# Top-32 attention with a PReLU MLP on one core: when pairs are prepared, how the MLP is paced, and two transposes moved from DMA to TensorE

## The chip, the core and the metric

The kernel runs on one core of a Trainium2 chip. A core has five engines with a queue each, which run in order and wait for each other through semaphores: TensorE (PE, matmul; its weight loads are listed as PEld), VectorE (DVE), ScalarE (ACT), GpSimd (POOL) and SyncE (SP, which here only issues DMAs). SBUF is the working memory, PSUM the small memory into which PE writes. The metric is the device time of one execution in microseconds (us); lower is better.

## What is computed

The reference is sparse attention followed by a two-layer MLP, all with random inputs:

```python
# q, k, v: (8 batches, 8 heads, 576 rows, 64)
scores = q @ k.T / sqrt(64)
kth = 32nd largest score of the row
scores = where(scores >= kth, scores, -1e9)
x = softmax(scores) @ v                      # -> (4608 tokens, 512)
h = x @ w_in                                 # (512, 2048)
g = maximum(h, 0) + alpha * minimum(h, 0)
out = g @ w_out                              # (2048, 512)
```

## The kernel before

**Pairs, row blocks, ticks.** Two heads of a batch form a pair; there are 32 pairs (four to a batch). A pair has nine row blocks of 128 score rows: four times 128 rows of each head and one block that holds the last 64 rows of both. That makes 288 row blocks. The program is one long list written out by hand (`manual_schedule`): a loop over ticks `n`, one row block to a tick, and each tick appends instructions to the five queues in a fixed order. Functions put into a calendar with `put(tick, engine, f)` are appended when the loop gets there (`run`). In the last four pairs (from tick 252) the row blocks are interleaved over the pairs, so that a chunk of 128 rows is complete for all heads of the batch early.

**A row block's way.** PE multiplies q and k (`ps`, L314), one unit of two row blocks at a time and a tick ahead. ACT copies the scores with a bias (`b`, L323), counts signs (`h`, L329) and takes the exponential (`e`, L334). POOL makes a sign word (`SG`, L339), DVE a keyed copy (`y`, L345) whose largest eight of each of six segments it finds (`C`, L355) and merges (`L`, L370 and L372). Seven ticks after its scores DVE compares the row with its limit (`mk`, L419), POOL multiplies mask and exponential (`w`, L429), and SP issues a transpose by DMA (`wT<-w`, L442). The last six row blocks use one fused DVE instruction instead (L426). PE multiplies `wT` with v (`pu`, L488), DVE takes the reciprocal of the row sums (`rz`, L505, or L534 in the last batch), and ACT, or DVE in the last batch, scales the result into `xb`. A DMA transpose (`x_turn`, L551) makes `xT`, the MLP's input.

**Preparation.** Before a pair's first row block its q, k and v are loaded (`load`, `load_v`, on SP's queue) and `prep_plan` spreads 17 steps over about 16 ticks ahead of `BASE[p]`: PE transposes q and k (`pq`, `pk`, `pt`), forms k's products (`pg`) and a statistic (`pr`, `st`), with ACT copies between them (`qkT`, `GK`) and DVE steps behind them (`P`, L226, and `sq`, L251 on). `BASE[p]` is 9p for the first 28 pairs, and 247, 250, 254 and 258 for the last four.

**MLP.** PReLU is split into a Relu part and a linear part, so that the second layer is `relu(h) @ (w_out * (1 - alpha)) + x @ (w_in @ (w_out * alpha))`. The matrix in the second term (`w_id_b`) is made once, by four bursts of 16 matmuls (`pl`, L596) and four ACT copies (L600). Tokens are taken in blocks of 512 or 128. A block is a list of steps in the deque `back`: `ph` steps (four matmuls of 512 columns each, or 16 of 128, L635) with an ACT Relu (L641), and `pz` steps, three to 128 tokens (20 matmuls in all, L649 and L653) with an ACT copy (L658) and a DMA out. A step's PE part goes into one tick and its ACT part to the head of the next. Up to tick 251 every tick takes one step; from tick 252 on a credit of 1.9 a tick (2.4 from tick 288) is spent at 0.9 for a `ph` and 1.5 for a `pz` step. `feed` appends a batch's blocks eight ticks after its last weights.

**The end.** After the last row block the remaining chunks of the last batch pass through `av_last`, `rz_last`, `out_last` and `x_turn`, and their MLP steps are appended to `back` two ticks after that.

Of the kernel before, what the change touches and what calls it, by code (L numbers as in the profile page):

```python
# [9 lines left out]
FP32 = mybir.dt.float32  # L10
BF16 = mybir.dt.bfloat16
# [5 lines left out]
S = 576  # L17
# [13 lines left out]
def kernel(  # L31
# [10 lines left out]
    nc = tc.nc  # L42
    B, H, S_, D = q.shape
# [5 lines left out]
    NPAIR = (B * H) // 2  # L49
# [15 lines left out]
    nc.gpsimd.memset(warm, 0.0)  # L65
    nc.scalar.activation(warm, warm, AF.Exp, scale=1.0)
    make_identity(nc, ident_f)
    ones_f = const.tile([128, 1], FP32, name="ones_f")
    nc.gpsimd.memset(ones_f, 1.0)
    bones = const.tile([128, 2], BF16, name="bones")  # L70
# [86 lines left out]
    while n < NT:  # L157
# [2 lines left out]
            unit_of[n + i] = (n, m, i)  # L160
        units.append((n, m))
        n += m
    BASE = {p: TPP * p for p in range(P0)}
    BASE.update({P0: N0 - 5, P0 + 1: N0 - 2, P0 + 2: N0 + 2, P0 + 3: N0 + 6})

    def prep_plan(p):
        d = pairs[p]
# [253 lines left out]
    def weights(n, fused):  # L421
        p, j = ORDER[n]
        d, t = pairs[p], tiles.pop(n)
        dst = w_dst(n)
        if fused:
            nc.vector.scalar_tensor_tensor(out=dst, in0=t["b"], scalar=row_limit(n),  # L426
                                           in1=t["e"], op0=ALU.is_ge, op1=ALU.mult)
        else:
            nc.gpsimd.tensor_tensor(dst, t["mk"], t["e"], ALU.mult)  # L429
        if j == 8:  # L430
            d["wTm"] = prep.tile([128, 9, 128], BF16, name="wT", bufs=6)
            if fused:
                nc.vector.tensor_copy(d["wm"][:, S:640], d["wm"][:, 0:64])
            else:
                nc.gpsimd.tensor_tensor(d["wm"][:, S:640], t["mk"][:, 0:64], t["e"][:, 0:64],
                                        ALU.mult)
            nc.sync.dma_start_transpose(d["wTm"][:, 0:5, :], d["wm"])
            nc.sync.dma_start_transpose(d["wTm"][:, 5:9, :], d["wm"][:, 64:S])
        elif j % 2 == 1:
            wT = prep.tile([128, 9, 128], BF16, name="wT", bufs=6)  # L440
            d["wT", j // 2] = wT
            nc.sync.dma_start_transpose(wT, d["w2"])  # L442

    DDs, xb, xm = {}, {}, {}

# [91 lines left out]
    def out_last(i, g):  # L537
# [4 lines left out]
            dst[:, 256 * g:256 * g + 256].rearrange("p (s d) -> p s d", s=4), pu[0:m, :, 0:D],  # L542
            rz[0:m, 0:4].unsqueeze(2).to_broadcast([m, 4, D]), ALU.mult)

    def x_turn(b, chunks):
        for i in chunks:
            c0 = (b * S + 128 * i) % NX
            if b == B - 1:
                c0 = b * S % NX + (64 + 128 * i if i < 4 else 0)
            if i < 4:  # L550
                nc.sync.dma_start_transpose(xT[:, :, c0:c0 + 128], xb[b][:, i, :])  # L551
            else:
                nc.sync.dma_start_transpose(xT[:, :, c0:c0 + 64], xm[b])

    def weight_steps():
        hold = {}

        def alpha():
            a16 = mlp.tile([NFT, 128], FP32, name="a16", bufs=1)
            nc.sync.dma_start(a16, moe_alpha.rearrange("(t p) -> t p", p=128))  # L560
            hold["a16"] = a16

        def alpha1():
            aps = ps_m.tile([128, NFT], FP32, name="aps", tag="misc")
            nc.tensor.transpose(aps, hold["a16"], ident_f[0:NFT, 0:NFT])
            hold["aps"] = aps
            hold["inT"] = mlp.tile([128, NKT, NFT, 128], BF16, name="w_inT", tag="gT", bufs=1)

        def alpha2():
            nc.scalar.copy(alpha_sb, hold["aps"])  # L570
            nc.gpsimd.tensor_scalar(alpha1m, alpha_sb, -1.0, 1.0, ALU.mult, ALU.add)

        def lin(f):
            return xT[:, f // 4, DM * (f % 4):DM * (f % 4 + 1)]

        def w_in(kk):
            for hf in range(0, DFF, 1024):
                nc.gpsimd.dma_start(w_in_b[:, kk, hf:hf + 1024],
                                    moe_w_in[kk * 128:(kk + 1) * 128, hf:hf + 1024])

        def w_in2(kk):
            nc.sync.dma_start_transpose(hold["inT"][:, kk, :, :], w_in_b[:, kk, :])

        def w_out(f):
            hold[f] = mlp.tile([128, DM], FP32, name="w_stage2", tag="stage", bufs=3)
            nc.sync.dma_start(hold[f], moe_w_out[f * 128:(f + 1) * 128, :])

        def w_out2(f):
            ws = hold.pop(f)
            nc.scalar.activation(w_out_b[:, f, :], ws, AF.Copy, scale=alpha1m[:, f:f + 1])  # L590
            nc.scalar.activation(lin(f), ws, AF.Copy, scale=alpha_sb[:, f:f + 1])

        def w_id(kk):
            hold["pl"] = pl = ps_m.tile([128, DM], FP32, name="pl", tag="misc")
            for f in range(NFT):
                nc.tensor.matmul(pl, hold["inT"][:, kk, f, :], lin(f),  # L596
                                 start=(f == 0), stop=(f == NFT - 1))

        def w_id2(kk):
            nc.scalar.copy(w_id_b[:, kk, :], hold["pl"])  # L600

        yield alpha, None
        yield (lambda: None), None
        yield (lambda: (alpha1(), w_out(0), w_out(1))), alpha2
        for f in range(NFT):
            yield ((lambda f=f: (w_out(f + 2) if f + 2 < NFT else None,
                                 w_in(f // 2) if f < 8 and f % 2 == 0 else None)),
                   (lambda f=f: w_out2(f)))
            yield (lambda: None), (lambda f=f: w_in2(f // 2) if f < 8 and f % 2 == 1 else None)
        for kk in range(NKT):  # L610
            yield (lambda kk=kk: w_id(kk)), (lambda kk=kk: w_id2(kk))

    banks = [0, 0]

# [8 lines left out]
    def mlp_steps(t0, tb):  # L623
# [16 lines left out]
        def ph_act(f):  # L640
            nc.scalar.activation(hold["gT"][:, f:f + fpp, 0:tb], hold.pop(f), AF.Relu)  # L641
# [22 lines left out]
                nc.sync.dma_start(out[o0:o0 + m, :], o_sb[0:m])  # L664

        for f in range(0, NFT, fpp):
            yield (lambda f=f: ph_step(f)), (lambda f=f: ph_act(f)), 0.9
        for r0 in range(0, tb, 128):
            m = min(128, tb - r0)
            for part in range(3):  # L670
                yield ((lambda r0=r0, m=m, part=part: pz_step(r0, m, part)),
                       (lambda r0=r0, m=m: pz_act(r0, m)) if part == 2 else None, 1.5)

    blocks = []
    for i in range(0, 6 * S, 2 * S):
# [4 lines left out]
    last.update({i: (t7 + 64 + 128 * i, 128) for i in range(4)})  # L680
    assert sum(x[1] for x in blocks + list(last.values())) == NTOK

    PE_TICK = 1.9
    LAG_S, LAG_M, LAG_W = 2, 3, 7
    NW = NT - 6

# [1 line left out]
    with tc.manual_schedule(engines={E.PE, E.Activation, E.DVE, E.Pool, E.SP}):  # L688
        cal = {}

        def put(tick, eng, f):
            cal.setdefault((tick, eng), []).append(f)
# [15 lines left out]
        def tail_of(n, wn):  # L708
            wp, wj = ORDER[wn]
            b = wp // KPB  # L710
            if wp < P0:
                if wj == 3:
                    put(n + 3, "pe", lambda: av(wp, 0))
                    put(n + 4, "dve", lambda: av_rz(wp, 0))
                    put(n + 6, "act", lambda: av_out(wp, 0))
                if wj == 8:
                    put(n + 4, "pe", lambda: av(wp, 1))
                    put(n + 5, "dve", lambda: av_rz(wp, 1))
                    put(n + 7, "act", lambda: av_out(wp, 1))
                    if wp % KPB == KPB - 1:  # L720
                        put(n + 7, "end", lambda: x_turn(b, range(5)))
                        put(n + 8, "end", lambda: feed((b + 1) * S))
            elif (wj == 8 or wj % 2) and wp % 2:
                i, g = (wj // 2, (wp - P0) // 2)
                dt = 4 if n < NT else 2
                put(n + dt, "pe", lambda: av_last(i, g))
                put(n + dt + 1, "dve", lambda: rz_last(i, g))
                put(n + dt + 1, "dvx", lambda: out_last(i, g))
                if g == 1:
                    put(n + dt + 1, "dvx", lambda: x_turn(b, (i,)))  # L730
                    put(n + dt + 3, "end",
                        lambda: back.extend(mlp_steps(*last.pop(i))))

        load(0, nc.scalar)
# [7 lines left out]
            for eng in ("act", "pool", "pe", "dve"):  # L742
                run(t, eng)
        scores(0)
        back = deque((a, c, 1.0) for a, c in weight_steps())
        credit = 0.0
        after = None
        wdue, held = {}, []
# [3 lines left out]
        end = max(NT + 24, 0)  # L752
        while n < end or back or after:
            for p in range(2, NPAIR):
                if n == max(0, BASE[p] - (18 if p < P0 else 17)):
                    load(p)
                    plan(p)
                if n == max(0, BASE[p] - 13):
                    load_v(p)
# [20 lines left out]
            run(n, "act")  # L780
            if n >= 3 and n % 3 == 0 and n - 3 < NT:
                sel_a((n - 3) // 3)
            credit = min(credit, 0.0) + (2.4 if n >= NT else PE_TICK if n >= N0 else 0.0)
            first = n < N0
            while back and (first or credit > 0.0):
                first = False
                if after:
                    after()
                pe_f, after, cost = back.popleft()
                pe_f()  # L790
                credit -= cost if n >= N0 else 0.0
            run(n, "pe")
            due = wdue.get(n, ())
            for wn in due:
# [179 lines left out]
```

## Time and profile before

| | |
|---|---|
| median of 3 executions | 927.65 us (926.9 to 927.79) |
| profiled execution | 929.21 us, span from first to last instruction 927.4 us |
| DVE busy | 847.7 us (91%) |
| ACT busy | 810.4 us (87%) |
| PE busy | 752.0 us (81%) |
| POOL busy | 431.0 us (46%) |
| mean granted TensorE clock | 0.908 |

A row of the timeline gives start, duration, engine, source line, operation, output and inputs, and in brackets the idle time of the engine just before with what ended it. A row of the waits gives who waited for whom, the total in us, the number of times and the longest. A row of a stretch gives its borders and length, then for each engine its busy time and instruction count, the granted clock, the DMA engines' share and GB/s. Matmuls overlap, so PE's busy time is not PE at its peak. The shares of the whole span mix stages with different limits; each stage has to be read by itself.

### The profile page before, as it was taken

What the parts mean: (1) busy time and instruction counts of PE and PEld (TensorE: products, weight loads), DVE (VectorE), ACT (ScalarE), POOL (GpSimd) and SP (SyncE); (2) the same over time, 40 slices, a digit from 0 to 9 for tenths busy, and PEclk for the clock granted to TensorE, in tenths of its full rate; (3) what the DMA queues carried; (4) which work ended last, traced back from release to release, by engine and by line L of the source; (5) the groups of instructions that cost most, each with busy time, mean ns of one, the idle gap of its engine ahead of it and who ended that gap; (6) DMA issues with size and microseconds to landing.
All of it is one profiled execution on the core that took longest, in us unless ns stands there. A gap on an engine that the chain in (4) does not pass through costs nothing.

```text
span 927.4 us, 20789 instructions
## 1 busy us (share of the span) xinstructions
PE 752.0 (81%) x5702; PEld 448.4 (48%) x5779; DVE 847.7 (91%) x5305; ACT 810.4 (87%) x1873; POOL 431.0 (46%) x629
## 2 busy tenths in 40 slices
PE   5866797678977788878986889787986788989996
PEld 3544444344543445544553455544553444544564
DVE  3899969999999999999999999999999888999970
ACT  4999979799897999999897998999997988879842
POOL 0364534544554455555555454555554434455510
PEclk9565788799997999999977999999987999979999
DMA  6699634544556555564546546464456843353551
GB/s 149 121 174 200 132 65 86 105 93 91 124 106 111 92 103 110 115 115 93 126 99 124 95 88 126 97 125 94 106 126 103 146 85 74 76 101 62 115 94 45
DMA packets 343021, 99.52 MB, mean 107 GB/s; under 512 B 335200, under 2 KB 335216, under 8 KB 342896
## 3 DMA queue, kind: packets, MB, share of 16 engines
q1 hardware_dynamic: 340544, 95.71, 52.5%
q0 software_dynamic: 1152, 2.10, 1.6%
q8 instruction: 48, 0.79, 0.4%
q14 instruction: 77, 0.63, 0.2%
q10 hardware_dynamic: 1200, 0.30, 0.2%
HBM read 36.71 MB, written 9.44 MB: 50 GB/s over the span
## 4 chain that ended last, share of the span: by engine, by line
ACT 42%; PE 26%; DVE 24%; issue 3%; DMA 2%; POOL 1%; SPq 1%; ACTq 0%
ACT b L323 10%; ACT h L329 9%; ACT e L334 8%; DVE C L355 7%; PE ps L314 7%; PE pz L653 7%; PE ph L635 5%; ACT gT L641 4%; DVE mk L419 4%; DVE y L345 4%; DVE C L372 3%; DVE L L370 3%; ACT xb L517 2%; PE pz L649 2%; PE pg L206 2%
## 5 line engine op out<-in xcount | busy, mean ns | idle before, releaser
L429 POOL TENSOR_TENSOR w<-mk,e 128x576 bf16<-128x576 bf16 x250 | 319.2, 1277 | 375.3 <-DVE mk L419 208.3
L355 DVE MAX8 C<-y 128x8 f32<-128x96 f32 x1728 | 421.1, 244 | 0.1
L314 PE MATMUL ps<-qkT 64*128 64x288 f32 (+1 forms) x1280 | 255.9, 478 | 26.3 <-ACT b L323 26.1
L323 ACT ACTIVATE b<-ps,NT 128x576 f32<-128x576 f32 x288 | 201.5, 755 | 3.2 <-PE ps L314 3.2
L329 ACT ACTIVATE h<-b 128x576 bf16<-128x576 f32 x288 | 202.0, 701 | 2.0
L635 PE MATMUL ph<-xT,w_in_b 128*128 128x128 bf16 (+1 forms) x920 | 151.5, 302 | 54.4 <-ACT gT L641 27.2
L314 PEld LDWEIGHTS ps<-qkT 64*128 64x128 f32 (+1 forms) x1280 | 135.4, 195 | 86.4 <-ACT b L323 46.7
L334 ACT ACTIVATE e<-b 128x1152 bf16<-128x1152 f32 (+1 forms) x158 | 173.8, 1100 | 0.0
L370 DVE MAX8 L<-C 128x8 f32<-128x48 f32 x864 | 163.8, 190 | 0.1
L345 DVE TENSOR_SCALAR y<-b,SG 128x576 int32<-128x576 int32 x288 | 147.5, 512 | 10.0 <-POOL SG L339 9.4
L419 DVE TENSOR_SCALAR mk<-b,KP 128x576 bf16<-128x576 f32 x282 | 143.8, 510 | 0.0
L653 PE MATMUL pz<-w_out_b,gT 128*128 128x512 bf16 x551 | 134.2, 379 | 4.1 <-issue 3.0
L635 PEld LDWEIGHTS <-w_in_b 128*128 128x128 bf16 x960 | 70.8, 99 | 124.0 <-issue 93.9
L641 ACT ACTIVATE gT<-ph 128x512 bf16<-128x512 f32 x144 | 87.8, 618 | 41.8 <-PE ph L635 41.7
L372 DVE MATCH_REPLACE8 C<-L,C 128x48 f32<-128x48 f32 x576 | 109.1, 189 | 0.0
L653 PEld LDWEIGHTS <-gT 128*128 128x128 bf16 x576 | 52.7, 98 | 68.6 <-issue 13.1
L488 PE MATMUL pu<-v_bf,wT 128*128 128x65 bf16 (+1 forms) x1600 | 71.0, 201 | 11.0 <-DMA wT<-w 8.4
L339 POOL TENSOR_SCALAR SG<-S_all 128x1 int32<-128x1 f32 x288 | 65.2, 227 | 27.8 <-ACT h L329 27.5
L488 PEld LDWEIGHTS <-wT 128*128 128x128 bf16 (+1 forms) x1600 | 66.2, 105 | 24.6 <-DMA wT<-w 8.9
L429 POOL TENSOR_TENSOR wm<-mk,e 128x576 bf16<-128x576 bf16 x32 | 40.8, 1276 | 49.7 <-DVE mk L419 47.9
L329 ACT ACTIVATION_READ_ACCUMULATOR h<-b 128x1 f32 x288 | 61.6, 214 | 0.0
L658 ACT COPY o_sb<-pz 128x512 f32<-128x512 f32 x36 | 21.3, 591 | 39.4 <-PE pz L653 39.4
(102 smaller groups left out, 838.0 us busy)
## 6 DMA issues: line engine op xcount, KB each, us to landing
out_dram<-o_sb SPq DMA_DIRECT2D x35, 256.0 KB, 2.2
st_q<-in_q_dram SPq DMA_DIRECT2D x64, 128.0 KB, 2.9
st_v<-in_v_dram SPq DMA_DIRECT2D x64, 128.0 KB, 2.6
kst<-in_k_dram SPq DMA_DIRECT2D x62, 128.0 KB, 2.8
w_stage<-in_moe_w_out_dram SPq DMA_DIRECT2D x16, 256.0 KB, 3.1
w_in_b<-in_moe_w_in_dram POOLq DMA_DIRECT2D x8, 256.0 KB, 6.8
wT<-w SPq DMA_TRANSPOSE x128, 3.3
st_q<-in_q_dram SPq DMA_DIRECT2D x32, 32.0 KB, 2.8
```

Of the source, the lines that this page charges most:

```text
L314: nc.tensor.matmul(o_, l_, r_, start=True, stop=True)
L323: nc.scalar.activation(t["b"].rearrange("p (a c) -> p a c", a=2), t["ps"], AF.Identity, bias=NT0[:, p * TPP + j:p * TPP + j + 1], scale=ON ...
L329: nc.scalar.activation(h, tiles[n]["b"], AF.Sign, accum_out=S_all[:, n:n + 1])
L334: nc.scalar.activation(e, tiles[n0]["bu"], AF.Exp, scale=scl)
L345: nc.vector.tensor_scalar(t["y"].bitcast(I32), t["b"].bitcast(I32), FLIP, SG[:, n:n + 1], ALU.bitwise_xor, ALU.bitwise_xor)
L355: return [lambda g=g: nc.vector.max(out=C[:, n % TPP, g, :], in_=t["y"][:, g * SEG:(g + 1) * SEG]) for g in range(NSEG)]
L370: ops.append(lambda r=r, src=src: nc.vector.max(out=L[:, 8 * r:8 * r + 8], in_=src))
L419: nc.vector.tensor_scalar(t["mk"], t["b"], row_limit(n), None, ALU.is_ge)
L429: nc.gpsimd.tensor_tensor(dst, t["mk"], t["e"], ALU.mult)
L488: nc.tensor.matmul(o_, wT[:, 4 * side + c, cs], d["v"][:, 5 * side + c, :], start=(c == 0), stop=(c == 4))
L635: nc.tensor.matmul(hold[f][:, i, :], w_in_b[:, kk, (f + i) * 128:(f + i + 1) * 128], xT[:, kk, c0:c0 + tb], start=(kk == 0), stop=(kk == N ...
L653: nc.tensor.matmul(pz[0:m], hold["gT"][:, f, r0:r0 + m], w_out_b[:, f, :], start=False, stop=(f == NFT - 1))
```

## The change

- `BASE` becomes 9p for pairs 0 to 10 and 8p + 10 from pair 11 on (the last pair keeps 258). The loads come 18 ticks ahead of it for all pairs.
- MLP steps have two costs. Before tick 252 a credit of 1.0 a tick is spent at 1.0 for a `ph` and 0.7 for a `pz` step, so that `pz` steps go two, one, two, one to a tick; from tick 252 on costs and credits are as before. Blocks are fed nine ticks after a batch's last weights instead of eight.
- The linear matrix: each of the four bursts is followed by an empty step, and its ACT copy belongs to that step, one tick later.
- The last 128-row chunk of the last pair (row block 287) is transposed by nine PE transposes into PSUM with one DVE and one ACT copy back, in place of a DMA. The last 128 rows of `xb` are transposed by four PE transposes and one DVE copy, and their MLP steps are appended two ticks sooner. For both there is a second identity in bf16; the staging tile of alpha shares a ring with other tiles.

```diff
+    ident_b = const.tile([128, 128], BF16, name="ident_b")
+    nc.gpsimd.tensor_copy(ident_b, ident_f)
...
-    BASE = {p: TPP * p for p in range(P0)}
-    BASE.update({P0: N0 - 5, P0 + 1: N0 - 2, P0 + 2: N0 + 2, P0 + 3: N0 + 6})
+    BASE = {p: min(TPP * p, N0 + 6 - 8 * (P0 + 3 - p)) for p in range(NPAIR)}
...
-            nc.sync.dma_start_transpose(wT, d["w2"])
+            if n == NT - 1:
+                wa = ps_a.tile([128, 5, 128], BF16, name="wa", tag="pa")
+                wb = ps_m.tile([128, 4, 128], BF16, name="wb", tag="misc")
+                for c in range(9):
+                    nc.tensor.transpose(wa[:, c, :] if c < 5 else wb[:, c - 5, :],
+                                        d["w2"][:, 128 * c:128 * c + 128], ident_b)
+                nc.vector.tensor_copy(wT[:, 0:5, :], wa)
+                nc.scalar.copy(wT[:, 5:9, :], wb)
+            else:
+                nc.sync.dma_start_transpose(wT, d["w2"])
...
+    def x_turn_last(i):
+        c0 = (B - 1) * S % NX + 64 + 128 * i
+        xa = ps_a.tile([128, NKT, 128], BF16, name="xa", tag="pa")
+        for kt in range(NKT):
+            nc.tensor.transpose(xa[:, kt, :], xb[B - 1][:, i, 128 * kt:128 * kt + 128], ident_b)
+        nc.vector.tensor_copy(xT[:, :, c0:c0 + 128], xa)
...
-            a16 = mlp.tile([NFT, 128], FP32, name="a16", bufs=1)
+            a16 = mlp.tile([NFT, 128], FP32, name="a16", tag="stage", bufs=3)
...
-            yield (lambda kk=kk: w_id(kk)), (lambda kk=kk: w_id2(kk))
+            yield (lambda kk=kk: w_id(kk)), None
+            yield (lambda: None), (lambda kk=kk: w_id2(kk))
...
-            yield (lambda f=f: ph_step(f)), (lambda f=f: ph_act(f)), 0.9
+            yield (lambda f=f: ph_step(f)), (lambda f=f: ph_act(f)), (1.0, 0.9)
...
-                       (lambda r0=r0, m=m: pz_act(r0, m)) if part == 2 else None, 1.5)
+                       (lambda r0=r0, m=m: pz_act(r0, m)) if part == 2 else None, (0.7, 1.5))
...
-    PE_TICK = 1.9
+    LOAD_AT = 18
...
-                        put(n + 8, "end", lambda: feed((b + 1) * S))
+                        put(n + 9, "end", lambda: feed((b + 1) * S))
...
-                    put(n + dt + 1, "dvx", lambda: x_turn(b, (i,)))
-                    put(n + dt + 3, "end",
+                    fast = i == 3
+                    put(n + dt + 1, "dvx", lambda: x_turn_last(i) if fast else x_turn(b, (i,)))
+                    put(n + dt + (1 if fast else 3), "end",
                         lambda: back.extend(mlp_steps(*last.pop(i))))
...
-                if n == max(0, BASE[p] - (18 if p < P0 else 17)):
+                if n == max(0, BASE[p] - LOAD_AT):
...
-            credit = min(credit, 0.0) + (2.4 if n >= NT else PE_TICK if n >= N0 else 0.0)
-            first = n < N0
-            while back and (first or credit > 0.0):
-                first = False
+            late = n >= N0
+            credit = min(credit, 0.0) + (2.4 if n >= NT else 1.9 if late else 1.0)
+            while back and credit > 0.0:
                 if after:
                     after()
                 pe_f, after, cost = back.popleft()
                 pe_f()
-                credit -= cost if n >= N0 else 0.0
+                credit -= cost[late]
```

2 lines of the change are left out of this document (1 added, 1 removed).

## The prediction

> **What bounds the kernel now.** I read the busy shares first, then stretches of the span, then the waits of VectorE (DVE), ScalarE (ACT) and TensorE (PE), then the instructions in order of time. A "tick" is one row block; its start is seen as the start of one `y` instruction (L345), and the borders of the stretches below are such starts.
>
> ```profile
> PE 752.0 (81%) x5702; PEld 448.4 (48%) x5779; DVE 847.7 (91%) x5305; ACT 810.4 (87%) x1873; POOL 431.0 (46%) x629
> ```
>
> DVE is at 91%, so the question is where the other 79.7 us of the 927.4 us span lie. The stretches answer it (columns: borders, length, busy us of PE, PEld, DVE, ACT, POOL with instruction counts, granted clock, DMA share, GB/s):
>
> ```profile
> 120.00:160.00 40.00, 34.05 (x217) 19.49 (x221) 30.75 (x196) 31.08 (x76) 15.62 (x23) 0.90 0.35 70
> 281.16:328.99 47.83, 37.69 (x274) 21.42 (x281) 46.13 (x288) 41.61 (x100) 24.01 (x34) 0.92 0.60 98
> 328.99:364.95 35.96, 32.55 (x244) 18.34 (x247) 35.47 (x229) 33.48 (x79) 18.15 (x26) 1.00 0.57 114
> 387.76:433.81 46.05, 36.34 (x277) 20.81 (x282) 46.02 (x288) 44.49 (x106) 24.02 (x34) 1.00 0.55 107
> 469.77:492.56 22.79, 16.44 (x124) 11.09 (x120) 22.79 (x145) 22.70 (x57) 11.74 (x16) 0.72 0.53 108
> 716.79:802.41 85.62, 70.44 (x576) 41.08 (x584) 73.61 (x466) 73.76 (x177) 36.20 (x51) 0.98 0.52 97
> 826.30:885.94 59.64, 56.53 (x411) 30.47 (x419) 57.70 (x348) 50.28 (x100) 31.17 (x46) 0.96 0.49 89
> 885.94:921.90 35.96, 34.33 (x398) 24.25 (x400) 14.34 (x69) 12.68 (x22) 1.47 (x2) 1.00 0.34 73
> ```
>
> Row 5 holds eight ticks without MLP work: DVE never pauses, 22.79 / 8 = 2.85 us a tick. That is the floor of a tick. Row 2 is the 16 first-layer (`ph`) ticks of an MLP block, row 3 its 12 second-layer (`pz`) ticks: DVE idles 1.70 and 0.49 us. Row 4 is another `ph` phase: 0.03 us. Two places stand out: 9.25 us idle in row 1, where the linear matrix is made, and 12.0 us in row 6, where the last pairs are prepared and block 2816 is computed. From 826 us on PE is busy 90.9 of 95.6 us: the end follows PE, not DVE.
>
> **The linear matrix (gain 4.9).** Waits between 112 and 165 us:
>
> ```profile
> ACT w_id_b L600 <- PE pl L596: 8.8, 4, 3.3
> DVE P L226 <- PE pr L218: 4.1, 1, 4.1
> DVE rz L505 <- PE pu L488: 3.8, 1, 3.8
> DVE sq L251 <- ACT MM L247: 1.3, 1, 1.3
> ```
>
> Today four bursts of 16 matmuls stand in ticks 35 to 38 and ACT copies each at the head of the next tick, so it sits on PE for 8.8 us. Afterwards the bursts stand in 35, 37, 39, 41, the copies two ticks behind. The first burst still lies ahead of `pr` in tick 35's queue, so DVE's 4.1 us stay. The `pu` of tick 37 then has one burst ahead of it instead of three in a row, and `sq` none: 3.8 + 1.3 go, less 0.2 that `rz` may still wait. ACT's 8.8 us cost nothing by themselves, since DVE waits for something else. Bounds: 0 (the bursts stay the same size) to 9.2.
>
> **Preparation every eight row blocks (gain 9.8).** Pairs 28 to 31 have BASE 247, 250, 254, 258; they get 234, 242, 250, 258, and every pair from 11 on moves ahead (27: 243 to 226). Nothing is added. Row 6 (85.62 us) idles 12.0; an ordinary stretch of nearly that length, rows 2 and 3 (83.8 us), idles 2.2. I take the difference. Steps move past others on ACT, PE and DVE, and the loads (six for q and k, four for v) go earlier in SP's queue; as many as before, over more ticks, so I cost them at nothing while DVE covers a tick; bounds 0 to 1.0, the largest P wait in the ordinary phases. Bounds of the gain: 0 (the idle time belongs to block 2816's `pz`) to 12.0.
>
> **MLP blocks fed a tick later (gain 3.6).** In tick 159:
>
> ```profile
> 494.41 0.59 PE L635 MATMUL ph<-xT,w_in_b 128*128 128x512 bf16 x1 [4.75 <-DMA xT<-xb]
> 496.32 0.60 ACT L641 ACTIVATE gT<-ph 128x512 bf16<-128x512 f32 x1 [3.71 <-PE ph L635]
> ```
>
> The first `ph` waits 4.75 us for the transposed rows, with the scores of the next row blocks behind it in PE's queue, and ACT, whose queue has the Relu next, loses 3.71 us of its lead. One tick is 2.85 us: scores and preparation go first and ACT keeps most of the 3.71. The 1.70 us that DVE idles in such a phase (row 2) against 0.03 in a phase without that wait (row 4) is the price of the lost lead; three phases before row 6 have it (ticks 51, 87, 159), and I take 1.2 of 1.7 each. Bounds 0 to 5.1.
>
> **MLP paced by step length (cost 9.0).** Before tick 252 each tick takes one step. Now `ph` costs 1.0 and `pz` 0.7 of a credit of 1.0: `ph` stays at one a tick, `pz` goes 2, 1, 2, 1, and 12 steps take 8 ticks instead of 12. This is the part that can hurt. PE's pieces at full clock:
>
> ```profile
> 332.14 0.60 PE L175 MATMUL pq<-ident_f,st_q 128*128 128x128 f32 x4
> 332.57 0.80 PE L488 MATMUL pu<-v_bf,wT 128*128 128x65 bf16 x20
> 334.48 1.68 PE L653 MATMUL pz<-w_out_b,gT 128*128 128x512 bf16 x7
> 338.29 0.27 PE L196 MATMUL pt<-ident_f,st_q 64*128 64x64 f32 x1 [0.39 <-ACT qkT L192]
> 341.20 1.28 PE L206 MATMUL pg<-kst 128*128 128x130 f32 x10
> 345.86 0.43 PE L218 MATMUL pr<-qTb,GK 64*64 64x512 bf16 x4
> 350.32 1.24 PE L488 MATMUL pu<-v_bf,wT 128*128 128x65 bf16 x30
> 353.02 0.17 PE L234 MATMUL st<-bones,P 128*128 128x2 bf16 x1
> 353.45 1.24 PE L314 MATMUL ps<-qkT 64*128 64x288 f32 x8
> ...
> 900.30 3.45 PE pz L653 x16
> ```
>
> (The last line is from the chain of waits: 3.45 / 16 = 0.216 us a `pz` matmul.) In nine ticks PE does five `ps` (6.20), `pq` and its twin `pk` (1.20), `pt` with its twin (0.45), `pg` 1.28, `pr` 0.43, `st` 0.43 and two `pu` (2.04): 12.0, or 1.33 a tick. A new `pz` phase holds 80 matmuls: 80 x 0.216 + 8 x 1.33 = 17.3 + 10.7 = 28.0 us of PE in 8 x 2.85 = 22.8 us of DVE. PE falls 5.2 us behind. What DVE reads from PE (`pr`, `pu`, `st`) is then late; the lead of 3.7 us that the later feed leaves covers the rest. I take 5.2 - 3.7 = 1.5 us a phase and six phases before tick 252 (blocks 0, 512, 1152, 1664, 2304, 2816): 9.0. The two short blocks have one pair of such ticks each (5.2 / 4 = 1.3 us, covered). Bounds per phase: 0 and 5.2. After a phase PE catches up in MLP-free ticks, now 11 or 12 instead of 8, and 6 where there was 1.
>
> **The last chunk by PE (cost 1.7).** The removed transfers, in order of time, and what used them:
>
> ```profile
> 895.95 2.27 DVE L426 SCALAR_TENSOR_TENSOR w<-b,KP,e 128x576 bf16<-128x576 f32 x3
> 898.58 2.72 SPq L442 DMA_TRANSPOSE wT<-w  x2
> 903.59 0.80 PE L488 MATMUL pu<-v_bf,wT 128*128 128x65 bf16 x20
> 904.23 3.75 PE L635 MATMUL ph<-xT,w_in_b 128*128 128x128 bf16 x64
> 905.10 2.00 SPq L551 DMA_TRANSPOSE xT<-xb  x1
> 913.15 3.75 PE L635 MATMUL ph<-xT,w_in_b 128*128 128x128 bf16 x64
> ```
>
> Neither `pu` at 903.59 nor `ph` at 913.15 waited: PE came from other `pz` and `ph` work. So taking two transfers away gains nothing. What is added is PE work: 13 transposes of 128 columns at 3.75 / 64 = 0.059, 0.8 us. And a wait: the nine of `w2` stand in PE's queue in tick 292, with half of block 4224's `ph` behind them, and cannot start before `w` ends at 895.95 + 2.27 = 898.22.
>
> ```profile
> 895.06 1.06 PE L635 MATMUL ph<-xT,w_in_b 128*128 128x128 bf16 x16
> 895.96 0.80 PE L488 MATMUL pu<-v_bf,wT 128*128 128x65 bf16 x20
> ```
>
> Today `ph` step 0 and then `pu` of tick 291 end at 896.7. In the new order steps 0 and 1 follow that `pu`: 896.7 + 0.94 = 897.6, so PE waits 0.6. With 0.3 for the copies' latency, 1.7. DVE's and ACT's copies out of PSUM fall after their last row block, where both are mostly idle (row 8). Upper bound: `pq`'s f32 transposes, 0.60 / 4 = 0.15 each, 13 x 0.15 + 0.6 + 0.9 = 3.5; lower, if the 1.63 us that PE pauses in row 8 closed: 0.8 - 1.6 = -0.8. The Trainium skill, "TensorE: Matmul & The Clock Gate", Part 4, gives about 275 to 390 ns for one bf16 transpose, in one kernel's context or alone: by it the 13 would be an estimated 3.6 to 5.1 us and the sum 2.8 to 4.3 us later; no row here shows a bf16 one.
>
> **Small parts.** `ident_b` is one POOL copy before the first loads have landed; `alpha` in the `stage` ring is released by one transpose in tick 2; one SP issue less each. Nothing, bounds 0 to 0.5. The feed of block 3456 moves from tick 266 to 267; in PE's queue only scores that were ahead anyway lie between, so nothing, bounds 0 to 2.85.
>
> **Sum.** -4.9 - 9.8 - 3.6 + 9.0 + 1.7 = -7.6. The profiled execution took 929.21 us with a span of 927.4, 1.6 above the median of 927.65; the sum gives a span of 919.8 and a median of 920.0. What DVE gains before 826 us moves the whole PE-bound end with it, since that begins with batch 6's `xT`.
>
> **Rivals.**
> 1. *PE becomes the bound in `pz` phases (slower).* No lead is left, and each phase costs its full 5.2: 31.2 - 4.9 - 9.8 - 3.6 + 1.7 = +14.6, 942. For it: `pz` ticks today are 32.55 of 35.96 busy on PE. Against: DVE's reads have some slack. It decides from 16.6 / 6 = 2.8 us a phase.
> 2. *PE's lag is absorbed.* Phase cost 0: -16.6, 911. For it: only P waits in these phases today (row 3, 0.49).
> 3. *Longer pauses cool PE.* Stretches after a pause:
>
> ```profile
> 492.56:502.00 9.44, 7.37 (x30) 3.78 (x33) 9.44 (x58) 4.94 (x14) 4.66 (x7) 0.60 0.59 115
> 387.76:397.00 9.24, 7.00 (x41) 3.76 (x41) 9.24 (x57) 9.09 (x23) 4.66 (x7) 1.00 0.64 132
> ```
>
> After eight MLP-free ticks the clock is 0.60, after one 1.00. Ticks 124 and 196 would now start cold too: 2 x 1.67 = 3.3, and if the cold clock and not the wait for `xT` cost row 2 its 1.70, the 3.6 are not gained either: -0.7, 926.9. The Trainium skill, same page, section "HAM oscillation — how this bites in real kernels", says the same from the other side: pauses over about 3.4 us throttle PE again. The trace agrees for the long pauses.
> 4. *The idle time of row 6 is the MLP's.* Only 4 of the 9.8 come: -1.8, 925.8.
>
> **How the numbers follow.** 0.2% (1.9 us) is about what a measurement here can tell from no change. Forecast 0.40 (914 to 926), rival 1 0.22, rival 2 0.18, rival 3 0.10, rival 4 0.10. Rivals 3 and 4 lie near the border, which gives "same" 0.10 and faster 0.68. Range 911 to 934: rival 2's end, and halfway into rival 1.
>
> **What would show it.** Right: 120 to 160 us idles 4 to 5 us of DVE, with the 4.1 us `pr` wait left; the stretch after 717 us idles under 4; ACT's first Relu of a block no longer waits 3.7; PE never pauses after batch 6's `xT`, and the tail from the last `w` to the end grows by 1 to 2 us. Wrong: `rz` and P waits on PE over 2.8 us in each `pz` phase.

## The result and the profile after

The changed kernel takes 973.46 us (median of four executions, 970.73 to 975.14) against 927.72 us: a ratio of 1.049, 95% interval 1.046 to 1.052. It is 45.7 us slower, where 7.6 us faster was forecast. Its profiled execution has a span of 969.0 us, 41.6 more than before.

First the stretches of both kernels, cut at the same ticks (borders, length, busy time of PE, PEld, DVE, ACT and POOL, granted clock, DMA share, GB/s). Before: ticks 35 to 50 with the linear matrix, ticks 231 to 256 with the last pairs, and the tail.

```profile
118.16:174.57 56.41, 43.23 (x311) 25.31 (x310) 47.16 (x296) 47.25 (x112) 23.78 (x33) 0.86 0.39 78
704.19:795.86 91.67, 75.53 (x545) 42.06 (x556) 79.22 (x497) 75.06 (x182) 39.12 (x55) 0.94 0.55 102
889.12:927.30 38.18, 31.14 (x351) 21.42 (x352) 11.16 (x51) 10.70 (x18) 0.00 (x0) 0.95 0.32 69
```

After: the linear matrix, then `ph` ticks 87 to 102 and `pz` ticks 103 to 114, `ph` ticks 123 to 138 and `pz` ticks 139 to 150, the ticks 151 to 158 without MLP work, the last pairs, the tail.

```profile
118.99:169.67 50.68, 41.56 (x316) 24.69 (x314) 46.90 (x297) 46.74 (x112) 23.76 (x33) 0.90 0.43 86
276.31:324.44 48.13, 37.81 (x284) 21.53 (x280) 46.56 (x293) 44.19 (x105) 24.09 (x34) 0.96 0.56 103
324.44:367.20 42.76, 38.48 (x310) 22.54 (x310) 36.73 (x230) 34.78 (x84) 18.23 (x26) 1.00 0.51 109
395.25:447.87 52.62, 41.84 (x279) 22.27 (x277) 47.04 (x292) 44.88 (x106) 24.10 (x34) 0.86 0.51 89
447.87:491.27 43.40, 35.93 (x258) 19.70 (x257) 35.79 (x227) 34.02 (x81) 18.20 (x26) 0.92 0.50 100
491.27:514.22 22.95, 17.59 (x128) 12.26 (x128) 22.95 (x147) 21.74 (x53) 11.73 (x16) 0.70 0.48 97
753.12:835.68 82.56, 70.18 (x495) 37.68 (x496) 75.97 (x474) 70.74 (x170) 39.14 (x55) 0.94 0.47 92
928.79:968.96 40.17, 32.97 (x381) 23.02 (x378) 12.07 (x53) 11.68 (x20) 0.00 (x0) 0.97 0.26 61
```

The two ends come out near the forecast: the linear matrix gains 5.7, the last pairs 9.1, the tail loses 2.0. The loss lies wholly between them. The `ph` ticks 123 to 138 took 46.05 us and take 52.62, DVE idle 5.6 of them; `pz` ticks 139 to 150 take 43.40 for about 36, DVE idle 7.6. Only ticks without MLP work still run at 2.87 us each without a pause. Ticks 51 to 230 take 583.4 us in all (from 169.7 to 753.1) where they took 529.6: +53.8, which with -4.9 up to tick 51, -9.1 for the last pairs and +1.8 behind them makes the 41.6.

DVE's busy time grew by only 4.3 us (847.7 before, 852.0 after, from the pages), so it waits. The waits of DVE and PE over the whole span, first before, then after (who waited for whom, us in all, times, longest):

```profile
DVE P L226 <- PE pr L218: 14.4, 19, 4.1
DVE rz L505 <- PE pu L488: 11.1, 7, 3.8
DVE y L345 <- POOL SG L339: 9.4, 7, 2.9
DVE sq L251 <- ACT MM L247: 3.7, 4, 1.3
...
PE pr L218 <- DVE P L226: 1.7, 2, 0.9
```

```profile
DVE y L346 <- POOL SG L340: 25.6, 15, 3.2
DVE P L227 <- PE pr L219: 18.7, 20, 3.7
DVE rz L515 <- PE pu L498: 18.1, 21, 1.6
DVE sq L252 <- ACT MM L248: 12.5, 14, 1.7
...
PE pr L219 <- DVE P L227: 12.9, 8, 3.9
```

One of the eight waits in the last line, in the `ph` ticks, seen in the timeline of PE, ACT and DVE:

```profile
409.27 1.24 PE L498 MATMUL pu<-v_bf,wT 128*128 128x65 bf16 x30
411.41 0.41 PE L219 MATMUL pr<-qTb,GK 64*64 64x512 bf16 x2
415.73 0.26 PE L219 MATMUL pr<-qTb,GK 64*64 64x64 bf16 x2 [3.92 <-DVE P L227]
415.93 2.29 PE L315 MATMUL ps<-qkT 64*128 64x288 f32 x8
...
420.07 0.60 ACT L659 ACTIVATE gT<-ph 128x512 bf16<-128x512 f32 x1 [6.05 <-PE ph L653]
...
415.01 0.67 DVE L227 TENSOR_TENSOR P<-pr,qTb 128x512 bf16<-128x512 f32 x1
416.03 0.23 DVE L227 TENSOR_TENSOR P<-pr,qTb 128x64 bf16<-128x64 f32 x1 [0.35 <-PE pr L219]
```

`pr` has two pieces. The large one ends at 411.82, the small one starts at 415.73, right when `P` has read the large one (415.01 + 0.67). So a buffer was missing. In the code `pr` (both pieces), `st` and `pu` share a PSUM ring of two buffers (tag "pd"), and `pu` keeps one from its matmuls until ACT has scaled the result, three ticks later. PE stands 3.92 us with the next scores and the next `ph` in its queue, and ACT, next in order, loses 6.05. Under the old `BASE` of 9p, `pr` always comes at the same place of the nine-tick pattern, where by the code no `pu` lives. At a spacing of eight it moves one place with every pair, through all of them.

### The profile page after: what moved, and what is told of

The parts are those of the page before. It is cut to its first block, busy times and chain, and to the rows that moved or that the text cites. A ratio compares the mean times of both kernels' runs of the same rounds, so it can differ in the third digit from the quotient of the medians.

```text
span 969.0 us, 20882 instructions
## 1 busy us (share of the span) xinstructions
PE 783.9 (81%) x5792; PEld 460.4 (48%) x5792; DVE 852.0 (88%) x5307; ACT 814.2 (84%) x1874; POOL 431.6 (45%) x630
## 4 chain that ended last, share of the span: by engine, by line
PE 33%; ACT 31%; DVE 30%; issue 2%; POOL 1%; DMA 1%; SPq 0%; ACTq 0%; POOLq 0%
PE pz L671 10%; DVE C L356 9%; ACT b L324 8%; PE ps L315 8%; ACT h L330 6%; ACT e L335 5%; DVE y L346 4%; DVE mk L420 4%; PE ph L653 4%; ACT gT L659 4%; DVE C L373 3%; DVE L L371 3%; PE pz L667 3%; PE pu L498 3%; PE pg L207 2%; ACT xb L527 2%
## 5 line engine op out<-in xcount | busy, mean ns | idle before, releaser
L315 PE MATMUL ps<-qkT 64*128 64x288 f32 (+1 forms) x1280 | 264.2, 498 | 29.1 <-ACT b L324 28.9
L653 PE MATMUL ph<-xT,w_in_b 128*128 128x128 bf16 (+1 forms) x960 | 155.5, 306 | 40.1 <-ACT gT L659 33.2
L315 PEld LDWEIGHTS ps<-qkT 64*128 64x128 f32 (+1 forms) x1280 | 139.0, 205 | 94.4 <-ACT b L324 48.7
L671 PE MATMUL pz<-w_out_b,gT 128*128 128x512 bf16 x576 | 138.7, 385 | 0.0
L671 PEld LDWEIGHTS <-gT 128*128 128x128 bf16 x576 | 54.9, 99 | 71.6 <-issue 13.4
L207 PE MATMUL pg<-kst 128*128 128x130 f32 x320 | 54.7, 330 | 11.7 <-ACT qTb L202 11.7
```

The source lines that it names most:

```text
L315: nc.tensor.matmul(o_, l_, r_, start=True, stop=True)
L653: nc.tensor.matmul(hold[f][:, i, :], w_in_b[:, kk, (f + i) * 128:(f + i + 1) * 128], xT[:, kk, c0:c0 + tb], start=(kk == 0), stop=(kk == N ...
L671: nc.tensor.matmul(pz[0:m], hold["gT"][:, f, r0:r0 + m], w_out_b[:, f, :], start=False, stop=(f == NFT - 1))
```

## The experiments

Letters in the expectations. A: the MLP's pace overloads PE. B: the moved preparation meets the rest of the order badly. C: only both together lose. R: B's mechanism is the "pd" ring. D: it is the density, a pair's preparation in eight ticks instead of nine. Q: part of it is the order of ACT's copies and PE's steps, whatever the bank. Beside each median stands the length of ticks 51 to 230 in that run's trace, from `y` to `y`, because that stretch holds what is in dispute; the shortest length found for it is 521 us. Ticks 231 to 256 are less sure: `e5_both_back` and `e12_dma_tail` have the same code there and take 89.8 and 85.7 us in their traces, so a difference of about 4 us between two single traces proves nothing there.

### Taking back one part, and one part alone

`e1_base_back` and `e2_pace_back` are the changed kernel with one part taken back, `e3_base_alone` and `e4_pace_alone` the kernel before with that part alone. The edits, as they stand in the first two:

```diff
 # e1_base_back
-    BASE = {p: min(TPP * p, N0 + 6 - 8 * (P0 + 3 - p)) for p in range(NPAIR)}
+    BASE = {p: TPP * p for p in range(P0)}
+    BASE.update({P0: N0 - 5, P0 + 1: N0 - 2, P0 + 2: N0 + 2, P0 + 3: N0 + 6})
...
-                if n == max(0, BASE[p] - LOAD_AT):
+                if n == max(0, BASE[p] - (18 if p < P0 else 17)):
 # e2_pace_back: one step a tick before tick 252
-            while back and credit > 0.0:
+            first = not late
+            while back and (first or credit > 0.0):
+                first = False
...
-                credit -= cost[late]
+                credit -= cost[late] if late else 0.0
```

> The changed kernel with the old preparation times (BASE 9p, then 247, 250, 254, 258). Theory A (the two-one pz ticks overload PE): the loss stays, about 973 plus the 9 us of the last pairs' crowding, 975 to 982. Theory B (preparing every eight row blocks puts the preparation's steps out of step with the nine-tick pattern of the row blocks, and the engines then wait for each other): the loss goes, but for some 2 us for each of six MLP blocks (what block 0, still prepared at nine, cost in the changed kernel): 927.7 - 4.9 - 3.6 + 12 + 1.7 = about 933. Theory C (it takes both): about 933 too, told apart by the next run.

> The changed kernel with one MLP step a tick before tick 252, as before. Theory A: the loss goes and the gains show, about 927.7 - 4.9 - 9.8 - 3.6 + 1.7 = 911. Theory B: the stretches of first-layer steps, which idled some 15 us more on VectorE than before, stay slow, and so do the second-layer ones in part: 930 to 950. Theory C: about 911 to 918.

> The kernel before with preparation every eight row blocks alone. Theory A: the last pairs' crowding goes and nothing else, about 918. Theory B: 935 to 955. Theory C: 918 to 925.

> The kernel before with the new pace of MLP steps alone (blocks still fed after eight ticks). Theory A: the whole loss, 960 to 985. Theory B and C: some 2 to 3 us for each of six MLP blocks, about 940 to 946.

| run | median us | ratio to before, 95% | ticks 51 to 230 |
|---|---|---|---|
| before | 927.7 | | 529.6 |
| after | 973.46 | 1.046 to 1.052 | 583.4 |
| e1_base_back (pace new) | 940.25 | 1.009 to 1.016 | 544.4 |
| e2_pace_back (`BASE` new) | 939.81 | 1.010 to 1.018 | 553.8 |
| e3_base_alone | 960.09 | 1.030 to 1.036 | 568.9 |
| e4_pace_alone | 959.65 | 1.031 to 1.036 | 558.1 |

Each part costs by itself, some 32 us on the kernel before (960.09 and 959.65): C falls, and A and B both hold, each for a part of the loss and neither as its only cause. With both taken back:

```diff
 # e5_both_back: e1_base_back and e2_pace_back together
```

> The changed kernel with the old preparation times and the old pace; the later matrix copies, the later feed and the PE transposes remain. If the two parts cost what they cost alone (32 us each), 973.5 - 33 - 33.6 = 907, so the three small parts together gain some 20. If the parts lean on each other, near 927.7 - 4.9 - 3.6 + 1.7 = 921.

915.89 us, between the two forecasts, ratio 0.987 (0.985 to 0.990), and ticks 51 to 230 in 521.2 us with DVE idle for 0.5. What is left of the change (linear matrix, feed, tail) is a good one. On this kernel the new `BASE` costs 23.9 us and the new pace 24.4; both together cost 57.6, 9.3 more than the sum.

### What the pace does

In `pz` ticks 139 to 150 of the run with the new pace and the old `BASE` (`e1_base_back`), the stretch and then PE and DVE in order of time:

```profile
433.16:473.19 40.03, 33.52 (x248) 18.54 (x246) 35.75 (x230) 33.84 (x79) 18.16 (x26) 0.99 0.49 109
```

```profile
434.84 1.02 PE L654 MATMUL ph<-xT,w_in_b 128*128 128x512 bf16 x4 [1.38 <-ACT gT L660]
438.42 1.02 PE L668 MATMUL pz<-w_id_b,xT 128*128 128x512 bf16 x4 [0.31 <-ACT gT L660]
...
450.07 1.47 PE L672 MATMUL pz<-w_out_b,gT 128*128 128x512 bf16 x6
451.47 0.43 PE L220 MATMUL pr<-qTb,GK 64*64 64x512 bf16 x4
452.21 1.02 PE L668 MATMUL pz<-w_id_b,xT 128*128 128x512 bf16 x4 [0.31 <-ACT o_sb L677]
...
451.91 0.82 DVE L228 TENSOR_TENSOR P<-pr,qTb 128x512 bf16<-128x512 f32 x2 [1.82 <-PE pr L220]
...
459.08 0.18 DVE L516 RECIPROCAL rz<-pu 128x4 f32<-128x4 f32 x1 [1.23 <-PE pu L499]
```

From 438.42 on PE works through, with two `pz` steps in a tick, and DVE waits for `pr` behind them and then for `pu`. In these ticks PE is the bound, as rival 1 had it. The phase costs 4.5 us here (40.03 against 35.50 in `e5_both_back`). With the old feed (`e4_pace_alone`) each of the five full `pz` phases up to tick 222 leaves DVE idle for 4.8 to 5.0 us, which is the surplus of 5.2 that the prediction worked out; with the later feed it is 2.3 to 4.3. The first row shows why the lead is not there to spend: 3.6 us before the first `pz`, PE itself waits for ACT.

The shorter phases also lengthen the stretches without MLP work: behind a long block from 8 ticks to 10 or 11, and behind a short one, ahead of the block that begins in tick 123 or 124, from one tick to six. The 9.41 us from the start of tick 123, first with the new pace, then with the old one (`e5_both_back`), and, also of `e5_both_back`, the 9.41 us from the start of tick 87, behind eight such ticks:

```profile
385.89:395.30 9.41, 6.97 (x32) 4.14 (x34) 9.41 (x58) 8.56 (x21) 4.66 (x7) 0.64 0.60 117
```

```profile
377.69:387.10 9.41, 8.56 (x44) 4.48 (x44) 9.41 (x58) 8.19 (x23) 4.66 (x7) 0.82 0.62 132
273.46:282.87 9.41, 7.83 (x37) 4.56 (x35) 9.41 (x58) 6.14 (x17) 4.66 (x7) 0.68 0.71 107
```

The clock granted is 0.64 instead of 0.82, and the `ph` ticks 123 to 138 take 47.27 us instead of 45.95: 1.3, at two such places 2.6. The Trainium skill, "TensorE: Matmul & The Clock Gate", section "HAM oscillation — how this bites in real kernels", says that an idle gap of more than about 3.4 us throttles PE again; the trace agrees in direction, here with ticks in which PE is partly busy (its longest pause between the last `pz` and the first `ph` is 2.40 us). That the clock is what costs the 1.3 us is not shown: the `ph` ticks 87 to 102 of `e5_both_back` begin at 0.68 and still take 45.95 us without a pause of DVE.

### Is it the ring?

R's test moves only the small piece of `pr` to the bank of `pq`, `pk`, `pt` and `pg`: on the kernel before with the new `BASE` (`e6_base_pr_bank`), on the changed kernel (`e7_after_pr_bank`), and on the changed kernel with the old pace (`e8_pace_back_pr_bank`).

```diff
-                pr = ps_d.tile([128, n1 - n0], FP32, name="pr", tag="pd")
+                pr = (ps_d if n0 == 0 else ps_a).tile([128, n1 - n0], FP32, name="pr",
+                                                      tag="pd" if n0 == 0 else "pa")
```

> The kernel before with preparation every eight row blocks, and the small second piece of pr in the PSUM buffer of the pa ring instead of the two-deep pd ring. Theory R (the ring: at nine, pr falls into the ticks in which no pu holds a pd buffer; at eight it meets one, so its second piece waits for VectorE to read the first, and TensorE's queue stands): the 32 us go and the crowding's 10 too, about 918. Theory D (denser preparation or its place in the row-block pattern costs by itself): stays at 945 to 960.

> The changed kernel with the second piece of pr in the pa ring. Theory R: 973.5 less the 32 of the preparation and less up to 10 of the crowding: 930 to 942. Theory D: 960 to 975.

> The changed kernel with the old pace and the second piece of pr in the pa ring. Theory R: 939.8 less 32 and less up to 10: 898 to 908, faster than the kernel before. Theory D: 930 to 940.

| run | median us | without the edit | ticks 51 to 230 | without |
|---|---|---|---|---|
| e6_base_pr_bank | 944.47 | 960.09 | 552.1 | 568.9 |
| e7_after_pr_bank | 953.65 | 973.46 | 564.7 | 583.4 |
| e8_pace_back_pr_bank | 930.26 | 939.81 | 537.6 | 553.8 |

R's forecasts were too low in all three runs, so the small piece of `pr` is not the whole of B. The edit takes 16 to 19 us out of ticks 51 to 230 each time, and PE's wait of `pr` for `P` (10.0 us in `e2_pace_back`) is gone; ahead of tick 51 it costs 2.7 to 2.9 us each time. It also takes away some of what the two parts cost beyond their sum. In ticks 51 to 230 that surplus is 583.4 - 544.4 - 553.8 + 521.2 = 6.4 without the edit and 564.7 - 544.4 - 537.6 + 521.2 = 3.9 with it. By the medians it goes from 9.3 to nothing (915.89 + 24.4 + 930.26 - 915.89 = 954.7, and 953.65 was measured), but the executions of `e8_pace_back_pr_bank` scatter from 923.3 to 936.6, with one more at 943.1, wider than any other's. So the ring carries half of `BASE`'s cost in these ticks (16.2 of 32.6) and some of the surplus; how much of the surplus is not settled.

### Place or density?

Two runs keep the spacing of nine and move the place. Built on `e5_both_back`:

```diff
 # e9_shift_four (e13_shift_eight: 8 in place of 4)
-    BASE = {p: TPP * p for p in range(P0)}
+    BASE = {p: TPP * p - min(4, max(0, p - 1)) for p in range(P0)}
```

> The changed kernel with the old preparation base and the old pacing (the one that took 915.9), and from the sixth pair on each pair prepared four ticks earlier, so that its pr comes at the fourth tick of the nine-tick pattern instead of the eighth, at the same spacing of nine. Only four pairs are spaced eight. Theory R (a live pu holds one of the two pd buffers when pr comes): every pair meets it, the second piece of pr waits for the first P as in the run with the new base alone, up to 2.6 us for each of some 26 pairs, so +30 to +68: 946 to 984. Theory D (it is the density, eight ticks for a pair's work instead of nine, that costs): only the four eight-tick pairs cost, 24.4 / 28 = 0.9 us each, +3.5: 917 to 921.

> The same with eight ticks earlier from the tenth pair on, so that pr comes at tick 0 of the pattern, where by the trace no pu is held. Theory R: only the eight pairs on the way (ticks 7 to 1 of the pattern) meet a live pu, and there about half of them, +4 to +18, and nothing from the tenth pair on: 920 to 934, idle time of DVE gone after tick 90. Theory D: eight pairs spaced eight at 0.9 us each, +7: 921 to 925; the two differ in the run with four ticks, and here in where the idle time lies.

(The 0.9 in these texts divides the pace's 24.4 by 28 pairs; rightly it is `BASE`'s 23.9 by the 21 pairs from pair 11 on, 1.1 each, which changes none of the readings.)

With `pr` four ticks earlier: 1005.92 us, ratio 1.084 (1.080 to 1.088), 90 us over `e5_both_back`, at the same density and above even R's 946 to 984. D falls as the cause of this; that a denser order costs something too is not excluded. With eight ticks: 945.30, above both forecasts. Of the 26.7 us by which its trace is longer than that of `e5_both_back`, 19.5 lie ahead of tick 79, where eight pairs walk to the new place (13.3 by tick 51, 6.2 from there), and only 1.8 in ticks 79 to 194, where every pair stands at the new place. So this place is nearly as good as the old one, as R had it; the walk costs 2.4 us a pair, which neither theory had (R 4 to 18 in all, D 7), and 4.4 more in ticks 195 to 222 are unexplained. With the small piece moved at the four-tick shift, and then `st` moved too (last edit also on the changed kernel with the old pace, and on the old pattern as a control):

```diff
 # e14_shift_four_pr_bank: e9_shift_four with the edit of pr
 # e16_shift_four_st_bank, e17_pace_back_st_bank, e18_both_back_st_bank: the edit of pr and
-            st = ps_d.tile([128, 2, TPP], FP32, name="st", tag="pd")
+            st = ps_a.tile([128, 2, TPP], FP32, name="st", tag="pa")
```

> The kernel with pairs prepared four ticks earlier at nine-tick spacing (1005.9), with pr's small second piece in the bank of pq, pk, pt and pg instead of the ring that pu uses. Theory R in its full form (only the second piece of pr makes pr and pu wait for one another): most of the 90 us goes, 916 to 930. Theory Q (half of the cost is elsewhere: one pd buffer is still taken by the large piece of pr and by st while pu lives, and the preparation's other steps on PE wait for copies that ACT does in another place of its order): about half stays, as it did with eight-tick spacing (14.4 of 23.9): 940 to 970.

> The four-tick shift with pr's second piece in the other bank (939.1), with st there too, so that of the preparation only the large piece of pr is left in the ring of pu. Theory R (the rest is the ring as well): the 23.2 us over the kernel prepared on the old pattern (915.9) shrink to under 8: 916 to 924. Theory Q (the rest is the order of ACT's copies and PE's steps, whatever the bank): 935 to 943.

> The changed kernel with the old pacing and pr's second piece in the other bank (930.3), with st there too. R: the remaining 14.4 us over 915.9 go to 0 to 5, or below nothing since the last pairs gain: 908 to 921. Q: 926 to 934.

> A control: the kernel with old base and old pacing (915.9), with pr's second piece and st in the other bank. There pr meets no live pu, so both theories expect 914 to 918; more would be the price of the bank itself (one buffer for pq, pk, pt, pg, pr's second piece and st), and would have to be taken off what the other runs show.

| run | median us | ticks 51 to 230 | 231 to 256 |
|---|---|---|---|
| e5_both_back | 915.89 | 521.2 | 89.8 |
| e9_shift_four | 1005.92 | 592.8 | 94.3 |
| e14_shift_four_pr_bank | 939.11 | 539.5 | 86.7 |
| e16_shift_four_st_bank | 945.38 | 538.7 | 92.4 |
| e8_pace_back_pr_bank | 930.26 | 537.6 | 80.4 |
| e17_pace_back_st_bank | 925.09 | 541.2 | 80.3 |
| e18_both_back_st_bank | 928.48 | 520.9 | 95.6 |

The waits of PE, first of `e9_shift_four`:

```profile
PE pu L499 <- DVE P L228: 47.2, 23, 4.7
PE ps L316 <- ACT b L325: 41.0, 40, 3.8
```

then of `e14_shift_four_pr_bank`, and of `e5_both_back`:

```profile
PE ps L317 <- ACT b L326: 53.1, 40, 4.6
PE ph L655 <- ACT gT L661: 25.9, 38, 1.9
PE pu L500 <- ACT xm L529: 8.3, 12, 0.8
```

```profile
PE ps L316 <- ACT b L325: 18.3, 19, 3.7
PE pu L499 <- DVE P L228: 10.7, 6, 3.4
```

At the four-tick place `pu` waits for a buffer that `pr` holds, 47.2 us in all instead of 10.7; with the small piece elsewhere that line is gone and 53.3 of 71.6 us in ticks 51 to 230 with it. Moving `st` as well gains nothing there (539.5 to 538.7, 537.6 to 541.2). So the rest, 16 to 20 us in both series, is not the ring through `st`, and R in its full form falls. The medians of the `st` runs mislead: by their control the move of both to the other bank costs 12.6 us as such. The control's trace, the shortest of its eleven executions, is 8.4 us longer than that of `e5_both_back`, none of it in ticks 51 to 230: 2.7 lie ahead of them (as with the small piece alone) and 5.8 in the last pairs, where traces differ by 4 anyway. What the rest is stays open. PE's waits for ACT's `b` grew from 18.3 to 53.1 us, which fits Q (PE and ACT waiting for each other in their orders), but no run changed ACT's order alone. The ring is not out of it either: in `e14_shift_four_pr_bank` `pu` waits 8.3 us, twelve times, for `xm`, ACT's last read of the `pu` before it, and in `e5_both_back` it never does. That fits a buffer still held by `pr`'s large piece, which no run moved.

### Single terms, and a better kernel

```diff
 # e11_feed_alone, on the kernel before
-                        put(n + 8, "end", lambda: feed((b + 1) * S))
+                        put(n + 9, "end", lambda: feed((b + 1) * S))
 # e12_dma_tail, on e5_both_back: the end as before
-            if n == NT - 1:
+            if n == NT:
...
-                    fast = i == 3
+                    fast = False
 # e15_spread_six, on e12_dma_tail, with the edit of pr (e10_spread_last: 7 in place of 6) and all loads 18 ticks ahead
+    BASE = {p: min(TPP * p, N0 + 6 - 6 * (P0 + 3 - p)) for p in range(NPAIR)}
```

> The kernel before with the MLP blocks fed one tick later (nine ticks after the chunk's last row block instead of eight) and nothing else. By the forecast's term 3.6 less: 924.1. By what the other runs leave for it (915.9 = 927.7 - 4.8 for the linear matrix + 1.9 for the tail - the feed, so 8.9 for it): 919.

> The kernel that took 915.9, with the end as before (last weights and outputs turned by DMA, fed two ticks later). By the forecast's term 1.7 less: 914.2; by the two traces' tails (38.2 against 40.2 us from the last y to the end) 2.0 less: 913.9. If the PE transposes gain on their own: 917 or more.

> The changed kernel with the old pacing, with the small second piece of pr in the other bank, with the transposes by DMA at the end as before, and the pairs prepared every nine row blocks up to the twentieth and every seven from there on, so that only the last eleven pairs leave the pattern. If the new base's gain in the last pairs (11.2 idle at ticks 231 to 256 down to about 2.6) can be had without its cost in the first twenty pairs: 915.9 - 8.6 - 2.0 for the tail + about 5 for eleven pairs at half of 0.9 = 905 to 912. If the cost lies in the last pairs themselves, 916 or more.

> As the run with seven-tick spacing for the last eleven pairs (916.9), with six ticks for the last seven pairs instead: fewer pairs off the pattern. If each pair off the pattern costs and the gain at ticks 231 to 256 stays (5.5 less idle time there than in the run with the end by DMA that took 914.3): 914.3 - 5.5 + up to 4 = 909 to 913. If fewer ticks for a pair cost what fewer pairs save: 914 to 918.

The feed alone: 919.35 us, ratio 0.992 (0.989 to 0.994), 8.8 us less than the kernel before, which took 928.12 beside it. The wait that it was to shorten, before and in that run:

```profile
PE ph L635 <- DMA xT<-xb: 23.4, 7, 5.4
```

```profile
PE ph L635 <- DMA xT<-xb: 3.2, 5, 1.2
```

The end by DMA: 914.26 against 915.89, 1.6, which alone is not clear of the noise (914.7 to 918.4 and 910.7 to 915.7); the tails in the two traces are 39.0 and 40.1 us.

Seven ticks for the last eleven pairs: 916.87. The last pairs take 77.4 us instead of 85.7 (`e12_dma_tail`), but ticks 195 to 222 lose 9.8 on the way. Six ticks for the last seven pairs: 910.01, ratio 0.982 (0.979 to 0.984), the lowest median here; the interval overlaps that of `e12_dma_tail` (0.981 to 0.987). Its ticks 51 to 230 take 522.9 us, 1.9 more than in `e12_dma_tail`, and the last pairs 80.4, 5.3 less. So the good of the new `BASE` seems to be had where it is needed, in the last pairs, with few pairs off the pattern; the 4.3 us between the two medians are about what the two runs scatter. Its busy times:

```profile
PE 744.1 (82%) x5705; PEld 446.0 (49%) x5779; DVE 844.8 (93%) x5305; ACT 808.1 (89%) x1873; POOL 430.9 (48%) x630
```

## Why the prediction was wrong

- **"Preparation every eight row blocks", the moved steps "at nothing", bounds 0 to 1.0: this step failed.** They cost 32.6 us in ticks 51 to 230 (553.8 - 521.2); half of it, 16.2, goes when the small piece of `pr` leaves the ring that it shares with `pu`, and the cause of the other half stays open. The bound was the largest P wait in ordinary phases, but in those phases `pr` stands at one place of the pattern, so they could not show what another place costs. The text counted what moves past what in the queues, and left out that `pr` and `pu` share two buffers whose lifetimes the move would bring together. Its condition, "while DVE covers a tick", is void once PE's queue stands.
- **Its gain of 9.8** was right in the stretch (9.1 after), but part of that belongs to the feed: it takes 1.9 to 6.0 there in the three runs that have it without the new `BASE` and with the old pace (91.7 to 86.0, 85.7 and 89.8). The terms of `BASE` and feed overlapped.
- **"MLP paced by step length", 1.5 a phase: mis-sized.** The surplus of 5.2 was right (4.8 to 5.0 idle with the old feed). Subtracting 3.7 was wrong: those 3.7 us were ACT's wait for a late `ph`, not work that PE has done ahead. Between 2.3 and 4.3 remained, 16.3 in the five phases up to tick 222. The short blocks, "covered", left DVE idle for 1.4 each, and the `ph` phases behind them for 1.2 each. In all 24.4 instead of 9.0.
- **The sum itself.** The two parts cost 9.3 more together than singly, in part through the ring; the sum had no such term.
- **"MLP blocks fed a tick later": right in kind, too small.** 8.8 for 3.6. The wait fell from 23.4 to 3.2 us, ticks 51 to 230 gained 8.1 and, in that one trace, the last pairs 5.6. The forecast counted three phases and left the rest to `BASE`.
- **"The linear matrix" was right:** 4.9, and 919.35 - 914.26 = 5.1 measured (feed alone against feed and linear matrix; 6.45 up to tick 51 in the two traces). The waits of `rz` and `sq` in that stretch are gone and the one of `P` for `pr` stays, with 3.7 us, as forecast.
- **"The last chunk by PE" was right in direction and about in size:** 1.7, and 1.6 by the medians of two runs that differ in nothing else, 1.1 by their tails. (The 2.0 between the tails of before and after hold the later feed too, which alone makes 38.3 into 39.1.) The PE part in order of time:

```profile
937.90 0.44 PE L447 MATMUL wa<-ident_b,w 128*128 128x128 bf16 x5
938.18 0.39 PE L447 MATMUL wb<-ident_b,w 128*128 128x128 bf16 x4
938.40 1.06 PE L653 MATMUL ph<-xT,w_in_b 128*128 128x128 bf16 x16
939.74 1.05 PE L653 MATMUL ph<-xT,w_in_b 128*128 128x128 bf16 x16 [0.28 <-ACT gT L659]
...
946.48 0.39 PE L559 MATMUL xa<-ident_b,xb 128*128 128x128 bf16 x4
946.70 1.50 PE L653 MATMUL ph<-xT,w_in_b 128*128 128x128 bf16 x24
```

Nine transposes hold PE for 0.50 us and four for 0.22: 0.055 each, near the 0.059 taken. The wait of 0.6 for `w` is not there: the first transpose starts right behind `ph`. In its place PE waits 0.28 for ACT a little later. The Trainium skill, "TensorE: Matmul & The Clock Gate", Part 4, has 275 to 390 ns for one; here that is no price in a row of them, and the measurement decides.

- **The rivals.** Rival 1 happened, but for `e4_pace_alone` rather than for the whole change; its 942 lacked the preparation's cost. Rival 2 is excluded. Rival 3 named the right two places, with 1.3 at each instead of 1.67, but the clock as their cause is not shown. Rival 4 is right in part, as the feed shows. None of them had the preparation as a cost, so all four together left out 23.9 us, or 33.2 with the surplus of both parts, of the 57.6 that the two parts cost.
- **"What would show it".** The linear matrix stretch idles 3.8 us, just under the 4 to 5 forecast, and the tail grows by 2.0, as forecast, but 0.8 of that comes with the feed. In the ticks of row 6 DVE idles 6.7 us, not under 4. "Wrong: `rz` and P waits on PE" is what the waits after show.

## What to carry to other kernels

When steps of one pipeline move against another that repeats with a fixed period, look up which PSUM ring each step's output shares and how long its neighbours live at the new place; a profile of the old place shows nothing of it. An engine's wait for a late producer is not a stock that a later overload can draw on: of 3.7 us counted on, 0.6 to 2.6 a phase were found. Where a denser order is wanted at the end alone, change the spacing there alone: six ticks for seven pairs kept the steady ticks at 522.9 us, where eight ticks for 21 pairs, with the same edit of `pr`, took 537.6.

## What had not been expected

- One place is worth 90 us: the same work at the same spacing, four ticks earlier, takes 1005.92 instead of 915.89 us.
- PE's bf16 transposes into PSUM run at 0.055 us each in a row, like matmuls of the same width (3.75 / 64 = 0.059).
- On the old pattern, moving `st` and the small piece of `pr` to the bank of `pq`, `pk`, `pt` and `pg` cost 12.6 us by the medians; of the 8.4 that the trace shows, none lie in ticks 51 to 230.
